# Where the first statistics, sums and normalizations stand ahead of the first w2 products

## The chip, the cores and the metric

The kernel runs on one core of one Trainium2 chip. A core has a matrix engine (TensorE, PE in the profile; its weight loads are listed apart as PEld), three engines for element work (VectorE or DVE, ScalarE or ACT, GpSimd or POOL), a queue that issues transfers (SyncE or SP), and 16 DMA engines. Each engine takes its instructions strictly in the order in which they were built, and waits at one whose inputs or whose buffer are not ready; what stands behind it waits too. The metric is the device time of a run in microseconds (us).

## The reference

The input x is 2048 x 576, in float32. It is normalized row by row, and two branches on the result are added to x:

```python
xn = _layernorm(x, axis=-1)
return x + _A_ref(xn, A_dft_seq_re, A_dft_seq_im, A_dft_hid_re, A_dft_hid_im) + _B_ref(xn, B_w1, B_w2)
# _A_ref:  a = xn @ dft_hid_re.T;  b = xn @ dft_hid_im.T;  y = dft_seq_re @ a - dft_seq_im @ b
# _B_ref:  h = max(xn @ w1, 0);    y = h @ w2              (w1: 576 x 4608, w2: 4608 x 576)
```

Branch A is a Fourier mixing written as matrix products; branch B is a two-layer perceptron with a rectifier.

## The kernel before

**Numbers.** PE multiplies float16. Every float32 operand is split into a high and a low float16 part, `split`: ACT writes the high part scaled by a power of two, then DVE writes the low part (lines 182 and 183). A product is the sum of three products of parts. The power of two comes from the largest magnitude of the operand: for the first block of weights DVE takes the maximum of each partition (`magnitude`, line 115, and line 575), PE transposes it (line 158), DVE reduces it (line 163), PE spreads it over the partitions (line 166), and DVE makes the scales with bit operations (lines 168 to 173).

**Stages.** x lies in 16 tiles of 128 rows, four tiles to a group. The hidden width 4608 is cut into 9 blocks of 512, and each step (block b, group g) computes the first layer for one block and one group, then the second. The second layer uses a scheme with seven products on quarters, whose operands are sums of quarters (`mlp1_out`, `sums_w2`). Results of the second layer are added into sums and written out by POOL with accumulating transfers (line 557). After all blocks comes branch A, which takes the last third of the time. The change touches only the opening: what happens before and around the first products with w2, that is steps (0, 0) and (0, 1).

**The opening, per tile t.** `stats` takes means and variances: two `bn_stats` on DVE per tile (line 200), an aggregate (line 203), a square root on ACT (line 210), and six small DVE operations (lines 211 to 222), the last of which is the shift `sh`. `normalize`, in the code N(t), writes the normalized tile in float32 on DVE (line 242) and its high part in float16 on ACT (line 243). `remainder`, E(t), subtracts the two for the low part (lines 247 and 250): on DVE for tile 0, on POOL for tiles 1 to 11. `transposes`, T(t), is ten transposes on PE into a PSUM buffer, and two copies by ACT into `xT` (lines 265 and 268). The PSUM pool of these buffers has two of them. One is held for a long stretch by the first two results of group 1 (`pq`); the transposes, the scale computations and later the w2 products take turns with what is left. `tile_by` is the first-layer products of one tile. `fill` is products whose result is not used. `sum_w2` sums magnitudes of w2 on ACT (line 630; the cast of the sums on DVE is line 640), and its scale leads to the splits of w2, which the first w2 product (line 540) needs. `mlp1_out` evacuates first-layer results: the rectified high parts on ACT (lines 350 and 353), low parts and sums on DVE (lines 354 to 358), then the high part of the sums on ACT (line 360) and the low part on DVE (line 361).

**What sets the order.** The kernel is written as one sequence of calls, from which a scheduler builds an order for each engine, by its own estimates; an instruction can move ahead of others on its engine where its inputs allow. `tc.issue_after(i)` keeps what is issued under it from being placed ahead of instruction i. Before the change this is used in the opening only for the statistics of tiles 12 to 15. `weave` mixes the steps of `stats` with other calls.

Of the kernel before, what the change touches and what calls it, by code (L numbers as in the profile page):

```python
# [13 lines left out]
AF = mybir.ActivationFunctionType  # L14
# [6 lines left out]
D = 576  # L21
# [28 lines left out]
def kernel(  # L50
# [139 lines left out]
    eps = const.tile([P, 1], F32, name="eps")  # L190
    nc.vector.memset(eps, EPS)

    def stats(ts):

        n = len(ts)
        mv = small.tile([P, n, 2], F32, tag=f"mv{n}", name=f"mv{ts[0]}")
        sts = [small.tile([P, 2, 6], F32, tag="st", name=f"st{t}", bufs=4) for t in ts]
        for t, st in zip(ts, sts):
            for j in range(2):
                nc.vector.bn_stats(st[:, j, :], acc[t][:, j * EH : (j + 1) * EH])  # L200
                yield
        for i, st in enumerate(sts):
            nc.vector.bn_aggr(mv[:, i], st.rearrange("p a b -> p (a b)"))
            yield
        r0, u, r, sh = (
            small.tile([P, n], F32, tag=f"{a}{n}", name=f"{a}_{ts[0]}") for a in ("r0", "u", "r", "sh")
        )
        m, v = mv[:, :, 0], mv[:, :, 1]
        stt = nc.vector.scalar_tensor_tensor
        nc.scalar.activation(u, v, AF.Sqrt, bias=eps)  # L210
        nc.vector.reciprocal(r0, u)
        yield

        stt(u, v, EPS, r0, ALU.add, ALU.mult)
        yield
        nc.vector.tensor_tensor(u, u, r0, ALU.mult)
        yield
        nc.vector.tensor_scalar(u, u, -0.5 * SX, 1.5 * SX, ALU.mult, ALU.add)
        yield
        nc.vector.tensor_tensor(r, u, r0, ALU.mult)  # L220
        yield
        stt(sh, m, -1.0, r, ALU.mult, ALU.mult)
        for i, t in enumerate(ts):
            means[t], factors[t], shifts[t] = mv[:, i, 0:1], r[:, i : i + 1], sh[:, i : i + 1]

# [8 lines left out]

    xns, xss = {}, {}

    def normalize(t, eng=nc.vector):
        stage = dbufs[t % 4]
        xn = xns[t] = stage[:, :D]

        xs = xss[t] = stage[:, D : 2 * D].bitcast(F16)
        eng.tensor_scalar(xn, acc[t], means[t], factors[t], ALU.subtract, ALU.mult)
        nc.scalar.activation(xs[:, :D], acc[t], AF.Identity, bias=shifts[t], scale=factors[t])  # L243

    def remainder(t, eng):
        xn, xs = xns[t], xss[t]
# [7 lines left out]
    def transposes(t):  # L254
        xs = xss[t]
        pt = ps2.tile([P, 2, 1024], F16, tag="ps2", name=f"pt{t}")
        for k in range(NKX):
            nc.tensor.transpose(
                pt[:, k // 8, (k % 8) * P : (k % 8 + 1) * P], xs[:, k * P : (k + 1) * P], ident
            )  # L260
        g, c = divmod(t, TG)

        nc.tensor.transpose(pt[:, 1, P : 2 * P], xs[:, D - P : D], ident)
        dst = xT[g][:, :, c * P : (c + 1) * P]
        nc.scalar.activation(
            dst[:, :8, :], pt[:, 0, :].rearrange("p (k t) -> p k t", t=P), AF.Copy
        )
        nc.scalar.activation(
            dst[:, 8:, :], pt[:, 1, : 2 * P].rearrange("p (k t) -> p k t", t=P), AF.Copy
        )  # L270

# [66 lines left out]
            ps.append(new_ps1(b, g, 0))  # L340
        mlp1_group(b, g, i, slice(0, G), ps[i], WK[:-1], start=(i == 0), stop=(i > 0))

    def mlp1_out(b, g, i, pa, pb):

        h = hs[b, g, i] = mlp.tile([P, 2, 7, GH], F16, tag="h", name=f"h{b}_{g}_{i}", bufs=4)
        st = mlp.tile([P, 5, GH], F32, tag="stage", name=f"s{b}_{g}_{i}")
        stt = nc.vector.scalar_tensor_tensor
        a11, a21, a12, a22 = pa[:, :GH], pa[:, GH:], pb[:, :GH], pb[:, GH:]
        r21, s1, s2, s3, s4 = (st[:, n] for n in range(5))
        nc.scalar.activation(r21, a21, AF.Relu)  # L350
        for q, src in ((slice(A11, A11 + 1), a11), (slice(A12, A22 + 1), pb)):
            hi, lo = (h[:, n, q].rearrange("p a b -> p (a b)") for n in range(2))
            nc.scalar.activation(hi, src, AF.Relu)
            stt(lo, src, 0.0, hi, ALU.max, ALU.subtract)  # L354
        stt(s3, a11, 0.0, r21, ALU.max, ALU.subtract)
        stt(s1, a22, 0.0, r21, ALU.max, ALU.add)
        stt(s2, a22, 0.0, s3, ALU.max, ALU.subtract)
        stt(s4, a12, 0.0, s2, ALU.max, ALU.subtract)
        hi, lo = (h[:, n, S1 : S4 + 1] for n in range(2))
        order["s"] = nc.scalar.activation(hi, st[:, 1:], AF.Copy).ins  # L360
        order["lo"] = nc.vector.tensor_tensor(lo, st[:, 1:], hi, ALU.subtract).ins  # L361
# [199 lines left out]
    def max_w1(b, f):  # L561

        i, r = divmod(f, 2)
        if f == 0:
            mx["w1", b], sc["w1", b], pw["w1", b] = cell("mw1"), cell("sw1"), cell("pw1")
        if r == 0:
            mx["f", b] = cell("mf", 2)
        with tc.issue_after(order["vfree"]) if b >= BB else nullcontext():
            magnitude(mx["f", b][:, r : r + 1], raws["w1", b, i][:, r * KT : (r + 1) * KT])
        if r:  # L570
            if b:
                m = mx["w1", b][:, i : i + 1]
            else:
                m = mx["b", i] = small.tile([P, 1], BF16, tag=f"mb{i}", name=f"mb{b}_{i}")
            nc.vector.tensor_reduce(m, mx["f", b], AX.X, ALU.max)
# [6 lines left out]
    def power_w1(b, i):  # L582
        s, p = (t["w1", b][:, i : i + 1] for t in (sc, pw))
        if b:
            yield from power(s, p, mx["w1", b][:, i : i + 1])
        else:
            power_pe(s, p, mx["b", i])
# [30 lines left out]
    def sum_w2(b, i):  # L618

        if i == 0:  # L620
            mx["w2", b], sc["w2", b], pw["w2", b] = cell("mw2"), cell("tw2"), cell("pw2")
        if b:
            junk = mlp.tile([P, 5, GH], F32, tag="stage", name=f"j{b}_{i}")
            junk = junk.rearrange("p a b -> p (a b)")[:, : 4 * EH]
            junk = junk.rearrange("p (q e) -> p q e", e=EH)
        else:
            new_w2(b, i)
            junk = w2s[b, i][:, 0, :4]
        with tc.issue_after(order["free"]) if b >= BB else nullcontext():
            nc.scalar.activation(  # L630
                junk, raws["w2", b, i], AF.Abs, scale=2.0**-10, accum_out=mx["w2", b][:, i : i + 1]
            )
# [133 lines left out]
    max_w1(0, 1)  # L766
    E(0, V)
    next(power_w1(0, 0), None)
    fill(24)
    T(0)  # L770
    fill(10, xss[0])
    split_w1(0, 0)
    tile_by(0, (0,), ps, WK0)
    split_w1(0, 1)
    tile_by(0, (1,), ps)
    weave(stats([1]))
    fill(8, xss[0])
    N(1)
    E(1, GP)
    T(1)  # L780
    fill(8, xss[1])
    s23 = stats([2, 3])
    weave(s23, no, lambda: max_w1(0, 2), no, lambda: max_w1(0, 3), lambda: next(power_w1(0, 1), None))
    tile_by(1, (0, 1), ps)
    split_w1(0, 2)
    N(2)
# [25 lines left out]
    T(6)  # L812
    tile_by(5, (0, 1), qs)
    T(7)
    weave(stats([8, 9, 10, 11]))
    for t in (8, 9, 10, 11):
        N(t)
        E(t, GP)
    mlp1_out(0, 0, 1, *ps[2:])
    tile_by(6, (0, 1), qs)  # L820
    w[3]()
    tile_by(7, (0, 1), qs)
# [424 lines left out]
```

## Time and profile before

| | |
|---|---|
| median of 3 runs | 1261.11 us (1260.76 to 1262.15) |
| profiled execution | 1262.99 us |
| its span on the core | 1261.1 us |
| PE busy | 1237.7 us |
| DVE busy | 1014.5 us |
| ACT busy | 716.9 us |
| POOL busy | 157.4 us |
| first w2 product starts | 58.77 us after the span's start |

How to read the rows below: a row of the timeline has its start, its duration, the engine, the line of the kernel before, the operation, what it writes and reads, and the shapes; "x4" merges four neighbours; a bracket at the end gives the time that the engine stood idle before it and what ended that. Instructions on an engine overlap a little, so the distance to the next start is less than the duration. In the chain of work that ended last a row has start, duration, and what the chain ran through.

### The profile page before, as it was taken

The numbers are of one execution on the slowest core, as the hardware profiler recorded it, in microseconds if no ns is written. First come the engines' busy times: TensorE is split into PE (matmuls) and PEld (weight loads), VectorE is DVE, ScalarE is ACT, GpSimd is POOL, SyncE is SP. The second block draws the span as 40 slices with busy tenths as digits, with TensorE's granted clock in tenths as the row PEclk, the third lists the DMA queues.
The fourth block names the chain that finished last, engine by engine and source line by source line (L and its number), as shares of the span: only waits on it lengthen the run. The fifth ranks groups of instructions, "written<-read, shape, count | busy, mean of one in ns | idle before, by whom it ended". The sixth has DMA issues, their size and how long they took to land.

```text
span 1261.1 us, 25526 instructions
## 1 busy us (share of the span) xinstructions
PE 1237.7 (98%) x10389; PEld 988.3 (78%) x10389; DVE 1014.5 (80%) x1921; ACT 716.9 (57%) x1210; POOL 157.4 (12%) x199
## 2 busy tenths in 40 slices
PE   8799999999999999999999999999999999999998
PEld 7565556888888888888888888877777777777776
DVE  8899987878878777788787878566888888787875
ACT  5866566676676666766766766544543433433342
POOL 2322211111111111212121212200000000000000
PEclk9999999999999999999999999999999999999999
DMA  9245657575657575756576766630054344434320
GB/s 339 80 81 95 122 117 157 116 134 136 133 123 171 120 154 116 136 139 135 118 160 134 156 127 120 116 84 1 1 172 124 124 125 142 144 109 145 117 87 20
DMA packets 65157, 155.46 MB, mean 123 GB/s; under 512 B 6544, under 2 KB 25488, under 8 KB 65040
## 3 DMA queue, kind: packets, MB, share of 16 engines
q1 hardware_dynamic: 42256, 111.36, 27.0%
q0 software_dynamic: 22784, 42.48, 25.1%
q8 instruction: 81, 1.33, 0.4%
q14 instruction: 36, 0.29, 0.1%
HBM read 106.63 MB, written 51.90 MB: 126 GB/s over the span
## 4 chain that ended last, share of the span: by engine, by line
PE 81%; DVE 10%; ACT 3%; DMA 3%; issue 2%; SPq 0%; POOL 0%; ACTq 0%; POOLq 0%; DVEq 0%
PE p L1179 24%; PE p L540 24%; PE bank L463 23%; PE pd L1060 8%; DMA raw_w<-in_w_dram 1%; PE p L310 1%; DVE w2s L183 1%; DVE h L361 1%; DMA acc<-in_x_dram 1%; DVE h L354 1%; DVE acc L409 1%; ACT w2s L182 1%; ACT dbuf L243 1%; DVE cs L183 0%; DVE dbuf L424 0%
## 5 line engine op out<-in xcount | busy, mean ns | idle before, releaser
L540 PE MATMUL p<-w2s,h 128*128 128x288 f16 x3024 | 408.2, 286 | 5.1 <-DVE acc L554 1.9
L540 PEld LDWEIGHTS <-h 128*128 128x128 f16 x3024 | 295.6, 98 | 80.6 <-issue 5.1
L1179 PE MATMUL p<-R,cs 128*128 128x288 f16 x2688 | 331.3, 287 | 2.3 <-DVE o L1185 2.3
L1179 PEld LDWEIGHTS <-cs 128*128 128x128 f16 x2688 | 263.7, 98 | 69.8 <-issue 2.5
L182 ACT ACTIVATE cs<-c,sc_c 128x1024 f16<-128x1024 f32 x112 | 128.2, 1148 | 196.2 <-PE p L1179 135.9
L183 DVE SCALAR_TENSOR_TENSOR cs<-c,sc_c,cs 128x1024 f16<-128x1024 f32 x112 | 143.4, 1282 | 41.3 <-ACT cs L182 40.9
L463 PEld LDWEIGHTS <-w1buf 128*128 128x128 f16 x1600 | 156.5, 98 | 21.6 <-issue 0.3
L463 PEld LDWEIGHTS <-dbuf 128*128 128x128 f16 x1200 | 117.4, 98 | 16.1
L463 PE MATMUL bank<-xT,w1buf 128*128 128x256 f16 x832 | 109.9, 273 | 0.0
L1060 PE MATMUL pd<-dbuf,xT 128*128 128x288 f16 x832 | 103.8, 286 | 0.0
L463 PE MATMUL bank<-acc,w1buf 128*128 128x256 f16 x768 | 102.1, 273 | 0.1
L1060 PEld LDWEIGHTS <-xT 128*128 128x128 f16 x832 | 80.8, 98 | 22.0 <-issue 1.9
L485 DVE TENSOR_TENSOR h<-s,h 128x1024 f16<-128x1024 f32 x56 | 68.5, 1223 | 33.9 <-ACT h L482 33.6
L557 POOL DMA_DIRECT2D spill<-dbuf x70 | 61.0, 875 | 234.2 <-DVE dbuf L554 202.6
L470 ACT ACTIVATE h<-acc 128x256 f16<-128x256 f32 x112 | 46.0, 411 | 76.7 <-DVE acc L493 71.4
L463 PE MATMUL bank<-xT,dbuf 128*128 128x256 f16 x624 | 82.5, 273 | 0.0
L482 ACT ACTIVATE h<-s 128x1024 f16<-128x1024 f32 x56 | 59.1, 1056 | 36.3 <-DVE s L477 35.6
L463 PE MATMUL bank<-acc,dbuf 128*128 128x256 f16 x576 | 76.6, 273 | 0.0
L1185 DVE SCALAR_TENSOR_TENSOR o<-p,us_c,o 128x288 f32<-128x288 f32 x112 | 57.5, 514 | 19.2 <-PE p L1179 19.2
L927 ACT ACTIVATE f<-f 128x1024 f32<-128x1024 f32 x64 | 66.9, 1046 | 0.4 <-DMA f<-in_cre_dram 0.3
L471 DVE SCALAR_TENSOR_TENSOR h<-acc,h 128x256 f16<-128x256 f32 x112 | 47.3, 422 | 20.6 <-ACT h L470 20.4
L551 ACT ACTIVATE dbuf<-p,c_ub 128x576 f32<-128x576 f32 x70 | 51.1, 731 | 15.2 <-PE p L540 14.9
(158 smaller groups left out, 1553.0 us busy)
## 6 DMA issues: line engine op xcount, KB each, us to landing
spill<-dbuf POOLq DMA_DIRECT2D x70, 288.0 KB, 5.3
f<-in_cre_dram SPq DMA_DIRECT2D x32, 512.0 KB, 5.5
f<-in_cim_dram SPq DMA_DIRECT2D x32, 512.0 KB, 5.0
c<-in_cre_dram SPq DMA_DIRECT2D x32, 512.0 KB, 4.4
c<-in_cim_dram SPq DMA_DIRECT2D x32, 512.0 KB, 4.8
spill<-sum POOLq DMA_DIRECT2D x42, 288.0 KB, 4.5
raw_w<-in_w_dram SPq DMA_DIRECT2D x17, 640.0 KB, 6.4
raw_w<-in_w_dram SPq DMA_DIRECT2D x18, 576.0 KB, 4.9
```

What stands on the lines that cost most here:

```text
L182: nc.scalar.activation(hi, src, AF.Copy, scale=s)
L183: nc.vector.scalar_tensor_tensor(lo, src, s, hi, ALU.mult, ALU.subtract)
L463: nc.tensor.matmul(ps, l, r, start=first and m == 0, stop=m == len(todo) - 1, skip_group_check=not first,)
L482: order["s"] = nc.scalar.activation(hi_s, st[:, 1:], AF.Copy).ins
L485: order["lo"] = nc.vector.tensor_tensor(lo_s, st[:, 1:], hi_s, ALU.subtract).ins
L540: nc.tensor.matmul(ps[:, c], h[:, x, qa, c * P : (c + 1) * P], w[:, y, qb], start=first and i == 0 and j == 0, stop=i == NQ - 1 and j == 2 ...
L551: freed(nc.scalar.activation(o, ps, AF.Copy, scale=us[b]))
L557: nc.gpsimd.dma_start(spill[g, row, col], o, accum_op=ALU.add)
L927: nc.scalar.activation(f, f, AF.Abs, scale=2.0**-10, accum_out=sums_c[:, n, q : q + 1])
L1060: nc.tensor.matmul(ps[j], xT[g][:, kx, c * P : (c + 1) * P], dsp[j][:, hl, k], start=(t % 2 == 0 and n == 0), stop=(t % 2 == 1 and n == le ...
L1179: nc.tensor.matmul(ps, w[:, a, k], r[:, c, rq], start=first and k == 0 and j == 0, stop=k == HK - 1 and j == 2, skip_group_check=not first,)
L1185: order["o"] = nc.vector.scalar_tensor_tensor(o, ps, us["c"][:, n : n + 1], o, ALU.mult, ALU.add).ins
```

## The change

A helper `behind(key)` holds an instruction behind one that was noted in `order`. Two kinds are now noted there: the last small step of `stats` (the shift, by its first tile) and the second copy of a tile's transposes (`xT`). With these, the opening is reordered:

- the statistics of tile 1 are called ahead of the split of the first w1 pair, and tile 1 is normalized ahead of its products;
- the maxima of the second w1 pair, and their scale, come after tile 1's shift and ahead of T(1), instead of in between the statistics of tiles 2 and 3; the statistics of tiles 2 and 3 are held behind tile 1's shift;
- the sums of w2 on ACT are held behind the copies of T(2) and T(3);
- the statistics of tiles 8 to 11 are held behind the shift of tiles 4 to 7;
- the ACT half of the normalization of tile 8 is held behind the copy of T(5), that of tiles 9 to 11 behind the copy of T(7), and the second evacuation of step (0, 0) on ACT behind the copy of T(6).

```diff
+    def behind(key):
+        return tc.issue_after(order[key]) if key in order else nullcontext()
-    def stats(ts):
+    def stats(ts, after=None):
...
-                nc.vector.bn_stats(st[:, j, :], acc[t][:, j * EH : (j + 1) * EH])
+                with behind(after):
+                    nc.vector.bn_stats(st[:, j, :], acc[t][:, j * EH : (j + 1) * EH])
...
-        stt(sh, m, -1.0, r, ALU.mult, ALU.mult)
+        order["sh", ts[0]] = stt(sh, m, -1.0, r, ALU.mult, ALU.mult).ins
...
-    def normalize(t, eng=nc.vector):
+    def normalize(t, eng=nc.vector, after=None):
...
-        nc.scalar.activation(xs[:, :D], acc[t], AF.Identity, bias=shifts[t], scale=factors[t])
+        with behind(after):
+            nc.scalar.activation(xs[:, :D], acc[t], AF.Identity, bias=shifts[t], scale=factors[t])
...
-        nc.scalar.activation(
+        order["xT", t] = nc.scalar.activation(
             dst[:, 8:, :], pt[:, 1, : 2 * P].rearrange("p (k t) -> p k t", t=P), AF.Copy
-        )
+        ).ins
...
-    def mlp1_out(b, g, i, pa, pb):
+    def mlp1_out(b, g, i, pa, pb, after=None):
...
-        nc.scalar.activation(r21, a21, AF.Relu)
+        with behind(after):
+            nc.scalar.activation(r21, a21, AF.Relu)
...
-            nc.scalar.activation(hi, src, AF.Relu)
+            with behind(after):
+                nc.scalar.activation(hi, src, AF.Relu)
...
-        with tc.issue_after(order["vfree"]) if b >= BB else nullcontext():
+        with behind("vfree" if b >= BB else ("sh", 1) if f > 1 else None):
             magnitude(mx["f", b][:, r : r + 1], raws["w1", b, i][:, r * KT : (r + 1) * KT])
...
-        with tc.issue_after(order["free"]) if b >= BB else nullcontext():
+        with behind("free" if b >= BB else None if b else ("xT", 2 + i)):
             nc.scalar.activation(
                 junk, raws["w2", b, i], AF.Abs, scale=2.0**-10, accum_out=mx["w2", b][:, i : i + 1]
             )
...
     next(power_w1(0, 0), None)
+    weave(stats([1]))
     fill(24)
     T(0)
     fill(10, xss[0])
     split_w1(0, 0)
     tile_by(0, (0,), ps, WK0)
     split_w1(0, 1)
-    tile_by(0, (1,), ps)
-    weave(stats([1]))
-    fill(8, xss[0])
     N(1)
     E(1, GP)
+    tile_by(0, (1,), ps)
+    fill(8, xss[0])
+    max_w1(0, 2)
+    max_w1(0, 3)
+    next(power_w1(0, 1), None)
     T(1)
     fill(8, xss[1])
-    s23 = stats([2, 3])
-    weave(s23, no, lambda: max_w1(0, 2), no, lambda: max_w1(0, 3), lambda: next(power_w1(0, 1), None))
+    weave(stats([2, 3], ("sh", 1)))
     tile_by(1, (0, 1), ps)
...
     T(7)
-    weave(stats([8, 9, 10, 11]))
-    for t in (8, 9, 10, 11):
-        N(t)
+    weave(stats([8, 9, 10, 11], ("sh", 4)))
+    N(8, after=("xT", 5))
+    E(8, GP)
+    mlp1_out(0, 0, 1, *ps[2:], after=("xT", 6))
+    for t in (9, 10, 11):
+        N(t, after=("xT", 7))
         E(t, GP)
-    mlp1_out(0, 0, 1, *ps[2:])
     tile_by(6, (0, 1), qs)
```

What the scheduler builds from this differs from the kernel before in the opening, and for a short way into the second step of block 0 and the first of block 1; the order of SP's transfers is the same. On ACT the square root of tile 1 now stands ahead of the copies of T(0), the sums of w2 ahead of the square root of tiles 4 to 7, and the high parts of tiles 8 to 11 together behind the copies of T(7). On DVE the eight `bn_stats` of tiles 8 to 11 stand behind the normalizations of tiles 4 to 7, and four evacuations of step (0, 1) stand between the small steps of the w2 scale. On PE the matmul of line 158 for the second w1 pair stands ahead of T(1). On POOL two reductions for block 1's scales move behind spill writes.

## The prediction

> **What bounds the kernel now.** I read the page's busy shares, then busy time by stretch, then what PE waited for in order of time, then the chain that ended last.
>
> ```profile
> PE 1237.7 (98%) x10389; PEld 988.3 (78%) x10389; DVE 1014.5 (80%) x1921; ACT 716.9 (57%) x1210; POOL 157.4 (12%) x199
> ```
> ```profile
> 0.00:60.00 60.00, 47.41 (x614) 39.59 (x615) 52.23 (x156) 42.39 (x71) 18.04 (x26) 0.97 0.61 209
> ```
> ```profile
> 66.00:118.00 52.00, 49.88 (x357) 32.57 (x355) 48.80 (x110) 34.81 (x57) 11.06 (x12) 1.00 0.48 75
> 118.00:191.00 73.00, 72.38 (x457) 43.66 (x457) 69.05 (x137) 41.78 (x72) 15.40 (x17) 1.00 0.62 120
> ```
> ```profile
> 58.77 1.02 PE L540 MATMUL p<-w2s,h 128*128 128x288 f16 x7 [0.96 <-ACT xT L268]
> ...
> 118.42 1.63 PE L540 MATMUL p<-w2s,h 128*128 128x288 f16 x12 [1.95 <-DVE acc L554]
> ```
> ```profile
> 99.23 1.60 DVE dbuf L183 x2
> 100.85 4.97 DMA raw_w<-in_w_dram
> ...
> 117.64 1.45 DVE acc L554 x2
> ```
> Columns of a stretch: its bounds and length, then busy PE, PEld, DVE, ACT, POOL, then clock and DMA. Over the span PE is full (98%), but the first 60 us have 12.6 us without PE work; there the kernel is a relay of DVE, ACT, POOL and PE. The first w2 product starts at 58.77. From 66 to 118 DVE is busy 94% of the time and PE 96%, and at 118.42 it is PE that waits, 1.95 us for DVE. The chain says why: a DVE split at 99.23 frees a buffer, a load of 4.97 follows, then the scale, then DVE work up to 117.64. All of this starts when DVE gets there. So two dates decide what the change is worth: when PE starts the w2 products (58.77), and when DVE has finished block 0's second tile group. PE has 1.95 us to spare against DVE at 118.42; a late DVE has nothing to spare.
>
> **The change, part one: tiles 1 to 3, and the start of 4 to 7.** Line numbers are those of the kernel before.
>
> ```profile
> 10.32 0.20 DVE L203 BATCH_NORM_AGGREGATE mv<-st 128x2 f32<-128x12 f32 x1
> ...
> 10.76 1.66 DVE L183 SCALAR_TENSOR_TENSOR w1buf<-raw_w,c_sw,w1buf 128x640 f16<-128x640 f32 x2
> ...
> 14.41 0.81 DVE L115 TENSOR_REDUCE c_mf<-raw_w 128x1 f32<-128x640 f32 x1
> ...
> 15.40 0.58 DVE L242 TENSOR_SCALAR dbuf<-acc,mv,r 128x576 f32<-128x576 f32 x1
> ...
> 20.47 0.56 DVE L242 TENSOR_SCALAR dbuf<-acc,mv,r 128x576 f32<-128x576 f32 x1
> ...
> 27.06 0.45 DVE L200 BATCH_NORM_STATS2 st<-acc 128x6 f32<-128x288 f32 x1
> 27.43 0.15 DVE L218 TENSOR_SCALAR u<-u 128x4 f32<-128x4 f32 x1
> ...
> 28.14 2.04 DVE L242 TENSOR_SCALAR dbuf<-acc,mv,r 128x576 f32<-128x576 f32 x4
> ```
> ```profile
> 16.48 1.15 ACT L630 ACTIVATE w2s<-raw_w 128x1152 f16<-128x1152 f32 x1
> ...
> 29.84 1.00 ACT L265 ACTIVATE xT<-pt 128x1024 f16<-128x1024 f16 x1
> 30.74 0.36 ACT L268 ACTIVATE xT<-pt 128x256 f16<-128x256 f16 x1
> 31.01 1.62 ACT L243 ACTIVATE dbuf<-acc,sh,r 128x576 f16<-128x576 f32 x2
> ```
> Up to the aggregate at 10.32 nothing moves. Then the two w1 splits (1.66) follow at once, and tile 1's small steps run back to back: from 10.44, 1.6 for the splits and about 1.0 for six steps that each wait for the one before. Tile 1 is normalized at 13.1, not 15.40: 2.3 us won. Its transposes win less, because in the new PE order the matmul on the second w1 scale stands ahead of them, and that scale now follows on DVE: 13.55 plus two reductions of 0.73 and a statistic of 0.37 (27.06 to 27.43) gives 15.4. So T(1) ends at 16.4, copied by 17.7.
>
> DVE then does four statistics, the scale, two aggregates, four more statistics, both splits of the second w1 pair, a ninth statistic: 13.55 + 1.46 + 4 x 0.37 + 0.7 + 4 x 0.37 + 2 x 0.79 + 0.37 + 0.4 of small steps = 21.0 for tiles 2 and 3, where the row has 20.47. So 0.6 lost there, while the second w1 split is done at 20.6.
>
> Here the first new wait bites. On ACT both sums of w2 now stand behind the copies of T(2) and T(3). Tile 2's ACT half runs 21.2 to 22.1, POOL's remainder to 23.6, T(2) to 24.05. Then ACT in order: copy 1.18, sum 1.2 (1.15 and its read-out), copy 1.18, sum 1.2, which is 28.8, and only then the square root for tiles 4 to 7. On DVE the cast of these sums (L640) stands ahead of that tile group's small steps, so DVE, free at 23.9, stands for 4.9 us. Six steps from 28.85 put the four normalizations at 30.2, where the row has 28.14: 2.0 us late, and the eight statistics of tiles 8 to 11 (8 x 0.37 = 3.0), done by then before, come after.
>
> One price here has no row: a reduction of DVE beside POOL's remainder of tile 1 (14.1 to 15.55). Of the rows beside POOL in the next fence but one, L355 reads one tensor in SBUF and is not held, L218 is held 0.9. I take nothing, since a reduction reads one tensor as L355 does; up to 1.0 late goes into the range.
>
> **Part two: the copies of T(5) to T(7).**
>
> ```profile
> 39.56 0.66 PE L258 MATMUL pt<-ident,dbuf 128*128 128x128 f16 x9 [2.60 <-ACT xT L268]
> ```
> ```profile
> 34.18 1.16 POOL L250 TENSOR_TENSOR dbuf<-dbuf 128x512 f16<-128x512 f32 x1
> 34.28 1.09 DVE L218 TENSOR_SCALAR u<-u 128x4 f32<-128x4 f32 x1
> ...
> 37.36 1.38 POOL L250 TENSOR_TENSOR dbuf<-dbuf 128x512 f16<-128x512 f32 x1
> ...
> 37.97 0.42 DVE L355 SCALAR_TENSOR_TENSOR s<-p,s 128x256 f32<-128x256 f32 x1
> ...
> 41.49 1.22 DVE L361 TENSOR_TENSOR h<-s,h 128x1024 f16<-128x1024 f32 x1
> ...
> 44.44 1.15 POOL L250 TENSOR_TENSOR dbuf<-dbuf 128x512 f16<-128x512 f32 x1
> ...
> 45.08 1.60 DVE L361 TENSOR_TENSOR h<-s,h 128x1024 f16<-128x1024 f32 x1 [1.57 <-ACT h L360]
> ```
> Before, T(6) waits 2.60 for T(5)'s copy, because ACT stood at tile 8's normalization. Now tile 8 comes behind that copy. ACT: four halves of tiles 4 to 7 from 30.27 (0.76 each) to 33.4, copy of T(4), two evacuations; T(5) leaves PE at 36.0, copied 37.3; T(6) starts at 37.5, not 39.56; 28 matmuls, T(7) at 39.75, copied 42.2. That is 2 to 4 us won on PE.
>
> It is given back to POOL's remainders of 8 to 11, which move behind it, to 43.5 and after: 4 x 1.47 = 5.9 us. The rows show what that does. L218 takes 0.15 alone and 1.09 beside POOL; L361 1.22 and 1.60. Both end as POOL's instruction ends. L355, whose one operand is PSUM, keeps 0.42. So DVE's normalizations, low parts and scale steps take turns with POOL; its PSUM evacuations do not. [...]
>
> Turn by turn from 43.5: POOL on tile 8 to 44.8; DVE tile 9's normalization to 45.3; evacuation; tile 10 to 46.1; POOL (9) to 47.1; tile 11 to 47.6; POOL (10) to 48.9; low part L361 to 50.0; POOL (11) to 51.25; then the w2 scale's steps, between which four evacuations of the next tile group now stand (0.33, 0.33, 0.60, 0.33).
>
> ```profile
> 46.69 0.41 DVE L163 TENSOR_REDUCE top<-pm 1x2 bf16<-1x256 f32 x1
> ...
> 49.19 0.23 DVE L652 TENSOR_SCALAR c_sw<-c_pw,c_inv 128x2 f32<-128x2 f32 x1
> ```
> The scale is ready at about 53.5, where the row has 49.42. Without any turn lost after tile 9 it is 51.15.
>
> **Part three: from the scale to the w2 products, and the sum.**
>
> ```profile
> 49.45 1.01 ACT L182 ACTIVATE w2s<-raw_w,c_sw 128x864 f16<-128x864 f32 x1 [0.45 <-DVE c_sw L652]
> 50.38 0.58 ACT L353 ACTIVATE h<-p 128x512 f16<-128x512 f32 x1
> ...
> 53.45 0.80 ACT L182 ACTIVATE w2s<-raw_w,c_sw 128x576 f16<-128x576 f32 x1
> ...
> 55.69 1.09 ACT L360 ACTIVATE h<-s 128x1024 f16<-128x1024 f32 x1
> ```
> ```profile
> 59.21 4.09 SPq L107 DMA_DIRECT2D raw_w<-in_w_dram  x2
> ```
> ```profile
> 63.53 0.81 DVE L115 TENSOR_REDUCE c_mf<-raw_w 128x1 f32<-128x640 f32 x1
> ...
> 65.80 1.23 DVE L361 TENSOR_TENSOR h<-s,h 128x1024 f16<-128x1024 f32 x1 [0.21 <-ACT h L360]
> ```
> ACT after the scale: two splits of 0.92, the high sums 0.95, T(9)'s copy 1.18, 0.47, T(10)'s first copy 0.91, a split 0.67, T(10)'s second copy 0.4: 6.45, and the first w2 product waits for that buffer. 53.5 + 6.45 = 60.0, against 58.77: 1.2 late. (Before it was 9.3 after the scale; the evacuations and T(8) now lie ahead of the scale, so part of the loss returns.)
>
> DVE from the scale's start at 53.3 has 14.3 us of work to the end of the second low part: three evacuations 1.0, two splits 2.1, eight sums 2.9, two low parts 2.3, four splits 2.9, evacuation 1.6, two reductions 1.46. The reductions need block 1's first w1 load, issued when the last split of the first w2 buffer ends, 62.3. Before, issue 59.21 to reduction 63.53 is 4.3 without a wait; now DVE asks 3.05 after the split: 0.8 to 1.3 of standing. End of the low part: 53.3 + 14.3 + 1.3 = 68.9 against 66.94 (65.80 and 1.14 to the next): 2.0 late.
>
> The later date decides. PE's 1.2 lies inside its 1.95 of spare time; DVE's 2.0 passes through the load at 100.85 to the wait at 118.42 and to the end, as after 118 both engines are full. SP issues the same transfers in the same order. On POOL the two reductions for block 1's w1 scales move behind the first and the fourth spill write:
> ```profile
> 69.22 1.40 POOL L557 DMA_DIRECT2D spill<-acc  x1 [3.12 <-DVE acc L554]
> ```
> At 1.40 each or less, plus the wait for the product, that costs nothing while the splits that need these scales stand some 15 us later (the second pair's at 99.23); without this cover it would be up to 3 x 1.40. Sum: +2.0. The profiled execution took 1262.99 around its span of 1261.1, so 1265.0 for it; it stands 1.88 above the median of the runs, 1261.11, so 1263.1 for the median. 0.2%, 2.5 us, is about what a measurement can tell from no change.
>
> **The rivals.**
> 1. The early copies win. PE has tile 7's transposes 4 us sooner; if POOL gets its turns during evacuations alone and the scale is ready by 49.4 as before, the first product is at 55.9 (2.9 early) and DVE, from 49.2, at 63.5 to 64.8, without and with the standing (3.4 to 2.1 early): 2.7 faster, 1258.4. For it: the 2.60 wait does go. Against: the two held rows above, and four evacuations ahead of the scale. It turns faster once the scale starts before 51.3 (51.3 + 15.6 = 66.9).
> 2. Slower by more: the load is the wall. If block 1's w1 takes 6.3 from issue to landing, as half of these do (row below), DVE stands 2.0 more: +4.0, 1265.1. The held reduction (+1.0) goes the same way.
> ```profile
> DMA to landing us min/median/max: 3.7/6.3/8.1
> ```
> Against: the same load before needed no more than 4.3.
> 3. The change is hidden: DVE's loss is made up in the idle time between 66 and 118 (52.00 less 48.80) and nothing is left: 1261.1. Against: most of that idle time follows the load at 100.85, which moves along.
>
> **How the numbers follow.** Forecast +2.0: 0.40 (its own range 1261.6 to 1264.8; 0.26 of it within 0.2%, 0.14 slower). Load as the wall: 0.28, slower. Early copies: 0.20 (0.18 faster, 0.02 within). Hidden: 0.12 (0.10 within, 0.02 faster). That gives faster 0.20, within 0.38, slower 0.42. The range runs from the early copies with part of the spread of their own (1257.8) to the load with part of the held reduction (1266.0).
>
> **What would show it.** Right: DVE idle some 5 us ahead of L640 near 24 to 29; T(6) near 37.5 without a long wait; DVE steps of 0.15 near 1 us long beside POOL between 44 and 52; the w2 scale near 53; the first w2 product near 60; DVE waiting about 1 us for block 1's w1. Wrong: a scale before 51, or a first product before 58; or statistics finished early, because the sums of w2 did not hold ACT.

## The result, and the profile after

| | before | after |
|---|---|---|
| median of 18 runs each, side by side | 1261.55 us (1259.41 to 1262.90) | 1265.10 us (1262.24 to 1270.06) |
| ratio, 95% interval | | 1.0030 (1.0022 to 1.0037) |
| profiled execution | 1262.99 us, span 1261.1 | 1266.75 us, span 1264.8 |
| mean granted clock of that execution | 0.997 | 0.995 |
| first w2 product starts | 58.77 | 60.46 |
| PE's wait for DVE near 120 ends | 118.42 | 121.42 |

The change makes the kernel 0.3% slower, 3.8 us by the ratio. The forecast was 1263.1 us, with a range of 1257.8 to 1266.0.

The timeline of DVE after the change. Line numbers are now those of the changed kernel: normalization is L247, the cast of the w2 sums L648, the w2 scale L660, the low part of the sums of quarters L369, an addition of a second-layer result L562.

```profile
12.58 0.58 DVE L247 TENSOR_SCALAR dbuf<-acc,mv,r 128x576 f32<-128x576 f32 x1
13.07 1.54 DVE L115 TENSOR_REDUCE c_mf<-raw_w 128x1 f32<-128x640 f32 x2
...
20.83 1.06 DVE L247 TENSOR_SCALAR dbuf<-acc,mv,r 128x576 f32<-128x576 f32 x2
...
28.66 0.17 DVE L648 CAST mb<-c_mw 128x2 bf16<-128x2 f32 x1 [5.36 <-ACT w2s L638]
...
29.94 2.05 DVE L247 TENSOR_SCALAR dbuf<-acc,mv,r 128x576 f32<-128x576 f32 x4
31.89 2.98 DVE L205 BATCH_NORM_STATS2 st<-acc 128x6 f32<-128x288 f32 x8
...
46.64 1.89 DVE L247 TENSOR_SCALAR dbuf<-acc,mv,r 128x576 f32<-128x576 f32 x2
...
51.35 1.05 DVE L652 TENSOR_TENSOR c_pp<-c_pw,c_pw 128x2 f32<-128x2 f32 x1
...
53.77 0.21 DVE L660 TENSOR_SCALAR c_sw<-c_pw,c_inv 128x2 f32<-128x2 f32 x1
...
66.79 1.55 DVE L115 TENSOR_REDUCE c_mf<-raw_w 128x1 f32<-128x640 f32 x2 [0.77 <-DMA raw_w<-in_w_dram]
68.25 1.22 DVE L369 TENSOR_TENSOR h<-s,h 128x1024 f16<-128x1024 f32 x1
69.38 1.17 DVE L205 BATCH_NORM_STATS2 st<-acc 128x6 f32<-128x288 f32 x3
71.17 0.82 DVE L562 SCALAR_TENSOR_TENSOR acc<-p,c_ub,acc 128x576 f32<-128x576 f32 x1 [0.61 <-PE p L548]
```

Read from the top: tile 1 is ready sooner (12.58), then DVE stands 5.36 us for the held sums of w2, then come tiles 4 to 7 and the eight statistics that before had been done by then. Between 45 and 52 DVE is held beside POOL, which works there from 44.64 to 52.39 with one gap of 0.49: two normalizations take 1.89 us, where the four at 29.94 take 2.05, and the short step of line 652 takes 1.05 and ends at 52.40, where the kernel before has 0.16. The scale is ready at 53.8. The low part of step (0, 1), counted to the start of the next instruction, ends at 69.38, against 66.94 before.

The timeline of PE:

```profile
38.59 0.67 PE L264 MATMUL pt<-ident,dbuf 128*128 128x128 f16 x9
...
58.12 0.66 PE L264 MATMUL pt<-ident,dbuf 128*128 128x128 f16 x9 [2.25 <-ACT xT L274]
...
60.46 1.84 PE L548 MATMUL p<-w2s,h 128*128 128x288 f16 x7 [1.62 <-ACT xT L274]
62.09 6.87 PE L316 MATMUL p<-xT,w1buf 128*128 128x512 f16 x28
...
121.42 3.04 PE L548 MATMUL p<-w2s,h 128*128 128x288 f16 x12 [2.10 <-DVE acc L562]
124.25 3.28 PE L316 MATMUL p<-xT,dbuf 128*128 128x512 f16 x13
```

T(6), at 38.59, no longer waits. But the seven first w2 products take 1.84 us where they took 1.02, and the twelve at 121.42 take 3.04 where they took 1.63: in this execution PE is slow right after it has stood, for 2.25 and 1.62 us ahead of the seven and for 2.10 ahead of the twelve. The same in busy time by stretch (the number behind the five engines is the granted clock):

```profile
30.00:35.00 5.00, 2.80 (x28) 2.46 (x29) 5.00 (x15) 4.34 (x7) 3.95 (x6) 0.77 1.00 289
35.00:40.00 5.00, 5.00 (x83) 5.00 (x81) 1.95 (x8) 3.28 (x8) 2.14 (x3) 0.89 0.41 134
55.00:60.00 5.00, 1.44 (x20) 1.20 (x20) 5.00 (x9) 5.00 (x8) 0.00 (x0) 1.00 0.02 3
60.00:65.00 5.00, 4.54 (x18) 2.23 (x18) 5.00 (x10) 3.58 (x7) 0.00 (x0) 0.66 0.20 48
...
119.00:121.40 2.40, 0.32 (x2) 0.04 (x1) 2.40 (x7) 2.37 (x4) 0.00 (x0) 1.00 0.00 0
121.40:124.00 2.60, 2.58 (x11) 1.57 (x11) 2.60 (x5) 0.83 (x2) 2.23 (x2) 0.51 0.35 23
```

PE is busy 1.44 of the five microseconds from 55 to 60, and from 60 to 65 it gets a clock of 0.66. It is busy 0.32 of 2.40 ahead of 121.4, and then gets 0.51.

### The profile page after: what moved, and what is told of

It is laid out like the page before. It is cut to its first block, busy times and chain, and to the rows that moved or that the text cites. A ratio compares the mean times of both kernels' runs of the same rounds, so it can differ in the third digit from the quotient of the medians.

```text
span 1264.8 us, 25525 instructions
## 1 busy us (share of the span) xinstructions
PE 1241.4 (98%) x10389; PEld 990.3 (78%) x10389; DVE 1013.6 (80%) x1921; ACT 718.1 (57%) x1210; POOL 158.2 (13%) x199
## 4 chain that ended last, share of the span: by engine, by line
PE 87%; DVE 6%; ACT 3%; issue 1%; DMA 1%; POOL 0%; SPq 0%; POOLq 0%; ACTq 0%; DVEq 0%
PE p L548 27%; PE p L1191 24%; PE bank L471 23%; PE pd L1072 8%; PE p L316 5%; ACT xT L271 1%; DVE cs L183 0%; DMA o<-spill 0%; DVE w2s L183 0%; ACT w2s L182 0%; DMA raw_w<-in_w_dram 0%; PE pd L1082 0%; DVE dbuf L247 0%; ACT f L939 0%; ACT h L368 0%
```

## The experiments: the change in its parts

All kernels were compared with the kernel before on their own chip, which gave medians of 1262.1 to 1262.3 us there; the ratios are to those runs. The change has three parts that can be taken apart: the order of tiles 1 to 3, the hold of the w2 sums behind T(2) and T(3), and the later places of tiles 8 to 11 and of the second evacuation.

**The sums not held.** The changed kernel, with one line as before:

```diff
-        with behind("free" if b >= BB else None if b else ("xT", 2 + i)):
+        with behind("free" if b >= BB else None):
```

> The changed kernel with one part undone: the sums of w2 on ACT are not held behind the copies of T(2) and T(3). The scheduler then puts both ahead of tile 2's normalization on ACT, and the square root of tiles 4 to 7 ahead of the copy of T(2). Theory A (the date at which DVE finishes the second low part of step (0, 1), 66.9 before and 69.4 after, passes to the end, and PE's clock adds to it): DVE no longer stands 5.4 us ahead of the cast, tiles 4 to 7 are normalized from about 25 instead of 29.9, and the low part ends 3 to 5 us sooner than after the change; the end at 1260.5 to 1262.5. Rival B (the loss is the lower PE clock after PE's waits at 55 to 60 and 119 to 121, not DVE's date): the waits of PE ahead of the first w2 product stay in kind, so 1264 to 1265.5. Rival C (the turns with POOL are the loss): these stay, so 1263.5 to 1265.

Measured: 1258.49 us, ratio 0.9965 (0.9953 to 0.9976). It is faster than both kernels. DVE:

```profile
23.66 0.49 DVE L648 CAST mb<-c_mw 128x2 bf16<-128x2 f32 x1
26.04 2.04 DVE L247 TENSOR_SCALAR dbuf<-acc,mv,r 128x576 f32<-128x576 f32 x4
...
43.03 0.70 DVE L660 TENSOR_SCALAR c_sw<-c_pw,c_inv 128x2 f32<-128x2 f32 x1
...
61.88 1.22 DVE L369 TENSOR_TENSOR h<-s,h 128x1024 f16<-128x1024 f32 x1
```

There is no stand ahead of the cast, tiles 4 to 7 are 3.9 us earlier, the scale 10.7 us. PE no longer waits for DVE near 120: the twelve products that stood at 121.42 start at 114.06 without a wait. By the ratios, this one hold costs 1.0030 less 0.9965, some 8 us, in the company of the other parts. Theory A has the direction right and underrates it; the two rivals fall.

**The order of tiles 1 to 3 alone.** The same, and tiles 8 to 11 and the second evacuation in their old places:

```diff
-    weave(stats([8, 9, 10, 11], ("sh", 4)))
-    N(8, after=("xT", 5))
-    E(8, GP)
-    mlp1_out(0, 0, 1, *ps[2:], after=("xT", 6))
-    for t in (9, 10, 11):
-        N(t, after=("xT", 7))
+    weave(stats([8, 9, 10, 11]))
+    for t in (8, 9, 10, 11):
+        N(t)
         E(t, GP)
+    mlp1_out(0, 0, 1, *ps[2:])
```

> The changed kernel with the sums of w2 not held and tiles 8 to 11 and the second evacuation of step (0, 0) in their old places: of the change, only the new order of tiles 1 to 3 is left. Theory A (the new places of the later tiles lose where the sums are held, since the statistics of tiles 8 to 11 then can no longer be done while DVE stands, and gain where they are free): no stand ahead of the cast, T(6) waits again about 2.6 us, scale at 45 to 47, low part 0 to 1.5 us earlier than 66.94, ratio to the kernel before 0.998 to 1.000 (1259.6 to 1262). Rival E (the order of tiles 1 to 3 is the whole gain of 0.9965 that the changed kernel without the hold has): ratio 0.996 to 0.9975.

Measured: 1259.38 us, ratio 0.9973 (0.9963 to 0.9984). That is rival E's range, though the interval just reaches theory A's (0.998): when the sums are free, the written places of the later tiles add nothing that can be told from zero. T(6), which I expected to wait again, starts at 35.46 without a wait.

```profile
26.81 2.04 DVE L247 TENSOR_SCALAR dbuf<-acc,mv,r 128x576 f32<-128x576 f32 x4
...
43.31 0.70 DVE L660 TENSOR_SCALAR c_sw<-c_pw,c_inv 128x2 f32<-128x2 f32 x1
...
62.25 1.22 DVE L369 TENSOR_TENSOR h<-s,h 128x1024 f16<-128x1024 f32 x1
```

But the gain is not that of the dates of tiles 1 to 3 alone. The scheduler moved the later tiles too, although nothing holds them here. On ACT the kernel before has tile 8's half ahead of the copy of T(5), and this run has it behind. First the kernel before (L243 the half, L265 the copy), then this run (L271 the copy, L249 the half):

```profile
35.94 0.87 ACT L243 ACTIVATE dbuf<-acc,sh,r 128x576 f16<-128x576 f32 x1 [1.41 <-DVE sh L222]
...
38.20 1.04 ACT L265 ACTIVATE xT<-pt 128x1024 f16<-128x1024 f16 x1
```

```profile
34.09 1.02 ACT L271 ACTIVATE xT<-pt 128x1024 f16<-128x1024 f16 x1
...
38.30 0.87 ACT L249 ACTIVATE dbuf<-acc,sh,r 128x576 f16<-128x576 f32 x1 [0.77 <-DVE sh L227]
```

Tiles 4 to 7 are normalized 1.3 us sooner than in the kernel before, but T(6) starts 4.1 us and the scale 6.1 us sooner. How much of the gain comes from either was not separated.

**The later tiles back, the sums held.** The edit shown last, made to the changed kernel with its hold:

> The changed kernel with tiles 8 to 11 (statistics, normalizations, remainders) and the second evacuation of step (0, 0) back in their old places. Theory A (most of the loss is the hold of the sums, the new place of the later tiles is worth little either way): DVE's stand of 5 us ahead of the cast stays, T(6) waits again about 2.6 us, the scale no longer takes turns with POOL but starts about 2 us later than 49.42, the second low part ends 1 to 2.5 us later than 66.94; time 1 to 3 us above the kernel before. Rival C (the later tiles' new place, with its turns between DVE and POOL, is the whole loss): low part within 0.5 of 66.94, the time within 0.5 us of the kernel before.

Measured: 1261.32 us, ratio 0.9994 (0.9985 to 1.0002). This is rival C: the low part starts at 65.89, against 65.80 in the kernel before, and the time cannot be told from that kernel's. With the hold in place, the later places cost 1.0030 less 0.9994, 4.5 us. Theory A's stand of 5 us is only 2.19, and the scale, at 46.63, comes earlier than 49.42, not later. The statistics of tiles 8 to 11 now fill the stand.

**The hold alone, in the kernel before:**

```diff
-        nc.scalar.activation(
+        order["xT", t] = nc.scalar.activation(
...
-        )
+        ).ins
...
-        with tc.issue_after(order["free"]) if b >= BB else nullcontext():
+        with tc.issue_after(order["free"] if b >= BB else order["xT", 2 + i]) if b >= BB or not b else nullcontext():
```

> The kernel before, with one part of the change alone: the sums of w2 on ACT held behind the copies of T(2) and T(3). Theory A (the hold makes DVE stand ahead of the cast of the sums, and the stand is passed on to tiles 4 to 7, the w2 scale and step (0, 1)): DVE idle 3 to 6 us ahead of the cast, tiles 4 to 7 normalized about 2 us later than 28.14, end of the second low part 1 to 2 us later than 66.94, 1 to 2.5 us slower than the kernel before. Rival B (the hold costs only together with the later tiles' new places): low part within 0.5 of 66.94, the time within 0.5 us of the kernel before.

Measured: 1262.81 us, ratio 1.0008 (0.9999 to 1.0017), so 0 to 2 us, which decides between neither theory. Theory A's stand does not appear: in this order the cast (30.86) comes behind eight more statistics and the normalization of tiles 4 to 7, so DVE has work while ACT is late. The low part still starts 0.9 us later than in the kernel before (66.74 for 65.80). What the hold costs depends on what DVE has left to do.

**The statistics of tiles 8 to 11 not held**, everything else as changed:

```diff
-    weave(stats([8, 9, 10, 11], ("sh", 4)))
+    weave(stats([8, 9, 10, 11]))
```

> The changed kernel, except that the statistics of tiles 8 to 11 are not held behind the shift of tiles 4 to 7. Theory A: they fill part of DVE's stand ahead of the cast, which falls from 5.36 to 2 to 3 us; after tiles 4 to 7 DVE has 3 us less to do, the scale is ready at 51 to 52.5 and the low part of step (0, 1) ends 1 to 2 us earlier than 69.38; ratio 0.9995 to 1.0015. Rival F (it is the turns between DVE and POOL and PE's clock that cost, and DVE has spare time after 30): scale within 0.5 of 53.77, ratio 1.002 to 1.004.

Measured: 1263.11 us, ratio 1.0006 (0.9998 to 1.0015): theory A, with the scale a little sooner than it had. DVE:

```profile
23.50 2.94 DVE L205 BATCH_NORM_STATS2 st<-acc 128x6 f32<-128x288 f32 x8
...
28.96 0.17 DVE L648 CAST mb<-c_mw 128x2 bf16<-128x2 f32 x1 [2.20 <-ACT w2s L638]
...
50.67 0.22 DVE L660 TENSOR_SCALAR c_sw<-c_pw,c_inv 128x2 f32<-128x2 f32 x1
```

The stand falls from 5.36 to 2.20 because the eight statistics (2.94) lie in it, and the scale is 3.1 us earlier. With the sums held, this second hold costs about 3 us (1.0030 less 1.0006). Also, tiles 8 to 11 are then normalized on DVE by 38.7, so that fewer of DVE's steps are left beside POOL's remainders at 45 to 49.

**POOL's remainders of tiles 9 to 11 left out**, to see what the turns with DVE cost:

```diff
     for t in (9, 10, 11):
         N(t, after=("xT", 7))
-        E(t, GP)
```

> The changed kernel with POOL's remainders of tiles 9 to 11 left out: the low parts of these three tiles are not computed, the transposes read what the buffers hold from earlier tiles, and the output is not the reference's for these rows. The order on ACT and DVE is that of the changed kernel. Theory A: the holds of DVE between 45 and 52.3 (0.7, 0.8, 0.6 and 0.9) go, the scale at about 51 instead of 53.8, the first w2 product at about 58, the low part at about 66.8, as before the change; the end at 1262 to 1263, the rest being PE's clock. Rival B: the waits of PE ahead of the products stay, so 1264.5 to 1265.5. Rival C (the turns with POOL are the whole loss): 1261 to 1261.7.

Measured: 1264.11 us, ratio 1.0012 (1.0004 to 1.0021), 2.3 us below the changed kernel by the ratios, and the scale is 1.6 us earlier (52.21). So leaving out the turns saves about 2 us. The time is in none of the three ranges, between theory A's and rival B's: the low part starts at 66.75, 1.0 us later than in the kernel before, but PE's wait near 120 ends at 120.85, 2.4 us later.

**The scale called early:**

```diff
     T(4)
+    w[3]()
...
     tile_by(6, (0, 1), qs)
-    w[3]()
     tile_by(7, (0, 1), qs)
```

> The changed kernel with the scale of w2 called after T(4) instead of after the products of tile 6. Its steps on DVE then stand between the normalizations and the statistics, while POOL works on tile 4, and the first w2 splits fill DVE's standing at 36.4 to 39.0. Theory A: the scale at about 34 instead of 53.8, the first w2 product at 55 to 57 instead of 60.5, the last low part of step (0, 1) 2 to 4 us sooner than 69.4; the end at 1261 to 1263. Rival B: as far as PE waits less ahead of the first products, 1.5 less: 1263.5. Rival C: the low part and the normalizations still take turns with POOL, only the scale steps' 1.5 goes: 1263.5.

Measured: 1265.18 us, ratio 1.0018 (1.0009 to 1.0026). Theory A's gain did not come; by the ratios the run is 1.5 us below the changed kernel, as rivals B and C had it, but the intervals overlap. The scale is ready at 39.33, 14 us earlier, but DVE then does the sums of w2 ahead of the low parts, and POOL's turns fall on them (POOL is busy for all of 50 to 55; in the changed kernel, with POOL idle, L670 takes 0.45 and L369 1.22):

```profile
51.15 1.41 DVE L670 TENSOR_TENSOR raw_w<-raw_w 128x288 f32<-128x288 f32 x1
...
52.81 2.10 DVE L369 TENSOR_TENSOR h<-s,h 128x1024 f16<-128x1024 f32 x1
...
69.66 1.23 DVE L369 TENSOR_TENSOR h<-s,h 128x1024 f16<-128x1024 f32 x1
```

The low part starts at 69.66, later than in the changed kernel (68.25), and yet the time is no longer. PE shows why:

```profile
61.61 1.84 PE L548 MATMUL p<-w2s,h 128*128 128x288 f16 x7 [0.81 <-ACT xT L274]
...
120.97 1.63 PE L548 MATMUL p<-w2s,h 128*128 128x288 f16 x12
```

The first w2 product comes 1.15 us later than in the changed kernel, and near 120 PE does not wait for DVE at all, so that the low part's date does not set the time there. So the date of the scale as such is not what the loss hangs on. The end of the low part sets the date near 120 only where PE waits for DVE there.

## The experiments: PE's clock

**PE kept busy** with 18 and 14 products whose result is not used, where the changed kernel stands for 2.25 and 1.62 us:

```diff
-        nc.tensor.transpose(pt[:, 1, P : 2 * P], xs[:, D - P : D], ident)
+        order["pt", t] = nc.tensor.transpose(pt[:, 1, P : 2 * P], xs[:, D - P : D], ident).ins
...
     T(10)
+    bank0 = new_ps1(0, 2, 0)
+
+    def keep(n, t):
+        for _ in range(n):
+            with tc.issue_after(order["pt", t]):
+                nc.tensor.matmul(
+                    bank0[:, :256], xss[9][:, :P], xss[9][:, :256], start=True, stop=True
+                )
+
+    keep(18, 10)
     T(11)
-    early = [mlp1(0, 2, 0), mlp1(0, 2, 1)]
+    keep(14, 11)
+    mlp1_group(0, 2, 0, slice(0, G), bank0)
+    early = [bank0, mlp1(0, 2, 1)]
```

> The changed kernel with 18 products whose result is not used between T(10) and T(11) and 14 between T(11) and the first w2 product (written to a bank that the next product starts anew), so that PE does not stand there; nothing else is moved in that stretch. Theory A: the granted clock stays at full from 58 to 65, the first seven w2 products take 1.0 instead of 1.84 and the 28 behind them 6.2 instead of 6.87, so PE is 1.5 ahead, but DVE's date stays at 69.4: PE's wait near 119 grows by about that, and the end moves by less than 0.7 us: 1264.4 to 1265.5. Rival B: the 1.5 passes to the end, with what the clock costs near 121 on top: 1261.5 to 1263.6. Rival C: as theory A.

Measured: 1264.90 us, ratio 1.0020 (1.0011 to 1.0030). The clock is 1.00 from 55 to 65, the first seven w2 products take 1.02, the 28 behind them 6.20, and DVE no longer waits for PE at L562. The ratio is 0.001 lower, which is some 1.2 us, but the intervals overlap. PE's wait near 120 still ends 2.6 us late:

```profile
120.98 1.63 PE L548 MATMUL p<-w2s,h 128*128 128x288 f16 x12 [1.85 <-DVE acc L562]
```

That is nearest to theory A, although the wait did not grow as it had it (1.85 for 2.10): PE, 1.0 us ahead of the changed kernel at 67.79, is only 0.2 ahead when it comes to the wait (119.1 for 119.3). So most of the loss, 0.20% of 0.30%, stays when PE has its full clock from 55 to 65; that the rest is the clock's is likely, but the times alone don't show it.

The same with POOL's remainders of tiles 9 to 11 left out:

```diff
     for t in (9, 10, 11):
         N(t, after=("xT", 7))
-        E(t, GP)
...
+    keep(18, 10)
     T(11)
...
+    keep(12, 11)
```

> The changed kernel without POOL's low parts of tiles 9 to 11 (they are not computed), and with 18 and 12 products whose result is not used behind the transposes of tiles 10 and 11. Without these products the low part of step (0, 1) was 1 us late, but PE's wait near 120 came 2.4 us late. Theory A (the difference is PE's lower clock at 60 to 65, passed on because DVE waits for the first product of PE): at full clock DVE's wait of 1.45 us for that product goes, PE's wait near 120 ends at 119.2 to 119.8, the time 0.4 to 1.2 us above the kernel before. Rival D (DVE's new order between 69 and 118 costs that itself): the wait still ends at 120.5 to 121, the time 1.5 to 2.5 us above the kernel before.

Measured: 1263.25 us, ratio 1.0006 (0.9997 to 1.0015). The time is theory A's, 0.8 us above the kernel before; the upper end of the interval, 1.9 us, still reaches rival D. The profiled execution does not decide it, since it is among the fastest of its kernel (1260.95 us; its wait near 120 ends at 117.50, sooner than either had it). Why it is so fast is worth a look. Up to the w2 scale DVE runs the same instructions in the same order as without the added products, yet not at the same time. First the execution without, then the one with:

```profile
30.52 2.04 DVE L247 TENSOR_SCALAR dbuf<-acc,mv,r 128x576 f32<-128x576 f32 x4
...
39.47 0.69 DVE L362 SCALAR_TENSOR_TENSOR h<-p,h 128x512 f16<-128x512 f32 x1 [2.25 <-ACT h L361]
...
52.21 0.22 DVE L660 TENSOR_SCALAR c_sw<-c_pw,c_inv 128x2 f32<-128x2 f32 x1
```

```profile
30.05 2.04 DVE L247 TENSOR_SCALAR dbuf<-acc,mv,r 128x576 f32<-128x576 f32 x4
...
37.71 0.69 DVE L362 SCALAR_TENSOR_TENSOR h<-p,h 128x512 f16<-128x512 f32 x1 [1.23 <-ACT h L361]
...
50.44 0.22 DVE L660 TENSOR_SCALAR c_sw<-c_pw,c_inv 128x2 f32<-128x2 f32 x1
```

The normalizations start 0.47 apart, the scales 1.77. In between lies PE's clock, again first without, then with:

```profile
30.00:35.00 5.00, 2.53 (x29) 2.02 (x27) 4.90 (x16) 3.77 (x5) 3.37 (x5) 0.80 1.10 326
35.00:40.00 5.00, 5.00 (x80) 5.00 (x79) 2.10 (x9) 3.45 (x9) 2.72 (x4) 0.86 0.28 102
```

```profile
30.00:35.00 5.00, 2.69 (x42) 2.35 (x43) 5.00 (x14) 4.49 (x7) 3.84 (x6) 1.00 1.05 308
35.00:40.00 5.00, 5.00 (x94) 5.00 (x92) 3.25 (x14) 4.46 (x11) 2.25 (x3) 1.00 0.39 130
```

PE waited in T(4) for 1.28, 0.28 and 0.89 us in the execution with the products, and no longer than 1.3, 0.3 and 0.9 in the one without, and yet the clock from 30 to 35 was 1.00 with and 0.80 without. Where it was 0.80, the evacuation at L362 and DVE's queue behind it, up to the scale, came another 1.3 us later.

**PE kept busy in both stretches**: 22 products ahead of T(4) were added to the 18 and 14, and T(4) was held behind them.

```diff
-    T(4)
+    for _ in range(22):
+        with tc.issue_after(order["pt", 3]):
+            last = nc.tensor.matmul(ps[3][:, 3 * P :], xss[3][:, :P], xss[3][:, :P], start=True, stop=True).ins
+    with tc.issue_after(last):
+        T(4)
```

> The changed kernel with products whose result is not used in both stretches in which PE stands: 22 ahead of the transposes of tile 4 (30 to 33), 18 and 14 behind those of tiles 10 and 11. If the lower clock at 30 to 40 (0.77 and 0.89 in the profiled execution) is what made T(5) to T(7) later than my prediction had them, and a part of the loss: clock 1.00 from 30 to 65, T(6) at 37.3 to 38.0, low part ending at 68 to 69.2, ratio 1.0005 to 1.0015, less spread between runs. If that clock costs nothing: as with the second stretch alone, ratio 1.0015 to 1.0025.

Measured: 1262.49 us, ratio 1.0008 (0.9996 to 1.0019), but as a test of the early clock it settles nothing. The products read a buffer that tile 7 also uses, so they waited until 33.62 and did not fill the stand (2.45 us); the clock was 1.00 in that execution all the same; and the new order of PE moved other work too, so that the low part started at 64.80, far earlier than expected, and PE did not wait for DVE near 120.

**The sums free and PE kept busy:**

```diff
-        with behind("free" if b >= BB else None if b else ("xT", 2 + i)):
+        with behind("free" if b >= BB else None):
...
+    keep(4, 10)
     T(11)
...
+    keep(20, 11)
```

> The changed kernel with the sums of w2 not held, and 4 and 20 products whose result is not used put behind the transposes of tiles 10 and 11, where PE otherwise stands for 2.18 us. If the lower clock after that stand (0.66 in 55 to 60, the 28 products of the first layer 7.79 us instead of 6.20) is paid in full, since PE no longer waits for DVE at 114: clock 1.00 from 50 to 65, 1.3 to 1.7 us faster than the run without these products, 1256.8 to 1257.2. If a later wait takes it up: 1258.2 to 1258.6, with a wait of about 1.5 us for DVE somewhere before 120.

Measured: 1256.73 us, ratio 0.9959 (0.9946 to 0.9972). By the medians that is 1.8 us below the same kernel without these products, as expected if the clock is paid in full; by the ratios it is 0.8 us, with five runs each and intervals that overlap, so the times alone don't settle it. The traces show the stand and the slow stretch gone. Stretches without the products, then PE with them:

```profile
50.00:55.00 5.00, 2.39 (x26) 1.67 (x25) 5.00 (x11) 5.00 (x9) 0.00 (x0) 1.00 0.06 11
55.00:60.00 5.00, 5.00 (x20) 2.13 (x18) 4.98 (x12) 1.45 (x3) 0.00 (x0) 0.66 0.71 239
```

```profile
52.19 2.35 PE L851 MATMUL p<-dbuf 128*128 128x256 f16 x20
54.54 0.53 PE L548 MATMUL p<-w2s,h 128*128 128x288 f16 x3
55.45 6.20 PE L316 MATMUL p<-xT,w1buf 128*128 128x512 f16 x28 [0.39 <-ACT xT L271]
```

Without them the 28 first-layer products behind the stand take 7.79 us. This is the fastest version found, 5.4 us below the kernel before on its chip by the medians.

## Why the prediction was right, and where its sum fell short

**The walk up to the low part held.** Tile 1 was put at 13.1 (12.58), tiles 2 and 3 at 21.0 (20.83), the stand at 4.9 us (5.36), tiles 4 to 7 at 30.2 (29.94), the scale at 53.5 (53.77), the first w2 product at 60.0 (60.46), DVE's wait for block 1's load at 0.8 to 1.3 (0.77), the end of the low part at 68.9 (69.38). The reductions beside POOL, priced at nothing, take 1.54 for two, 0.77 each, while POOL works from 13.66 to 15.08; the two at 66.79, with POOL idle, take 1.55: not held. That reading one tensor in SBUF is what spares them, as the price had it, no run shows: L218 reads one, too (`u<-u`), and took 1.09 for 0.15.

So the hold of the sums, the eight statistics left for later and the turns with POOL were the right mechanisms, and the experiments show each of them: 8 us for the hold in this company, 3 for the statistics, 2 for the turns (they overlap and don't add up). One reading of the rows was wrong: L361 at 45.08 does not end as POOL's instruction ends. That one ends at 45.59 and L361 at 46.68, so L361 was held only until 45.59 and then took its usual 1.1 us.

**What failed is the last step of the sum**, "DVE's 2.0 passes through the load at 100.85 to the wait at 118.42 and to the end, as after 118 both engines are full". The lag was 2.44 at the low part and 3.00 at the wait (121.42 against 118.42). At the next group of products it was 4.36 (124.25 against 119.89), since the twelve products took 2.83 to the next start instead of 1.47. At the end of the span it was 3.7. Two terms were missing:

- PE after a stand was priced at full clock. It ran at 0.51 from 121.4 to 124 in this execution; that alone is 1.4 us. "PE's 1.2 lies inside its 1.95 of spare time" fails in the same way: the stretch behind the first w2 product also ran slowly (6.87 for 6.20), and DVE waited 0.61 for its result (L562), about the growth from 2.44 to 3.00. In the profiled execution with PE kept busy there, that wait is gone and the lag does not grow: 2.75 at the low part, 2.56 at the wait. Behind the wait the clock is 1.00 in that execution too, though no products were added there.
- T(6) was put at 37.5 and came at 38.59, with PE at 0.77 and 0.89 from 30 to 40. In the run with the remainders left out and PE kept busy, whose profiled execution has a clock of 1.00 there, T(6) starts at 37.25. At the scale 0.3 of the 1.1 was left.

The forecast (1263.1) is 2.0 us short of the median (1265.1). Of these, 0.4 are the base: the prediction started from the median of three runs, 1261.11, and the median of 18 is 1261.55. How much of the rest is the clock on average is not shown. Over 18 runs the changed kernel's granted clock is 0.9952 in the mean, and 0.9962 to 0.9966 in three sets of 25 to 29 runs of the kernel before. If PE's 1238 us of work paid that difference in full, it would be 1.2 to 1.7 us. But it is not paid in full everywhere: with PE kept busy the mean is 0.9979, above that of the kernel before, and the time is still 0.20% longer. What that run leaves, 2.5 us (1.4 to 3.8), is close to the 2.0 that the prediction put on DVE.

The range held with some luck. The measured 1265.1 lies just above 1261.6 to 1264.8, which the prediction gave to its own mechanism. The upper end of the whole range was there for a late load and a held reduction, neither of which came; it covered a term that the sum did not have.

**The rivals.** The load as the wall gave almost the measured time (1265.1) by another mechanism: DVE stood 0.77 for the load, not 2.0 more. "The early copies win" fell for the change as it is: T(6) came 1 us earlier than before, and the scale at 53.8, far behind the 51.3 where it turns. With the sums free it holds: T(6) starts without a wait (34.79), the scale at 43.03 is ahead of 51.3, and the kernel is faster. That the change is hidden fell too.

**What the prediction had the wrong way round** is the worth of the first part. It counted tile 1 as 2.3 us won and tiles 2 and 3 as 0.6 lost, and then only followed the new wait. Without that wait, writing tiles 1 to 3 in the new order is worth 0.27%, together with what the scheduler then did with the later tiles: a gain that the hold, together with the held statistics, turned into a loss.

## What to carry to other kernels

An instruction held back on one engine was paid for here on the engine whose next instruction reads the result (ACT's sums, DVE's 5.36 us); look there for work that can fill the stand, and don't hold that work back too. A stand of PE cost its length and, in some executions, a lower clock behind it (down to 0.51 after 2.10 us), so a date for PE after a wait needs both terms. Where a change has several holds, price them apart: here a good reordering was hidden under one bad hold. And read the order that the scheduler built, since it may already do what a hold is meant to force, as with T(5)'s copy here.

## What the runs showed of the hardware

I had not expected that PE's clock is lower after stands of about 2 us, in some executions and not in others. After PE's wait near 120 the twelve products took 3.04 us after 2.10 (changed kernel), 2.25 after 2.18 (remainders left out) and 2.54 after 2.28 (statistics not held), and the clock from 118 to 124 was 0.79, 0.81 and 0.72. They took 1.63, at a clock of 1.00, after 1.85 (PE kept busy), 1.95 (kernel before) and 2.27 (remainders left out, PE kept busy). The waits in T(4), the longest of 1.28 to 1.30 us, went with a clock from 30 to 35 of 0.77 (changed kernel) and 0.80 (remainders left out), and of 1.00 (statistics not held; remainders left out, PE kept busy). What decides between the two, no run here settles.

Over all runs, filling the stands raised the mean granted clock in each of three pairs: from 0.9952 to 0.9979 for the changed kernel, from 0.9943 to 0.9977 with the remainders left out, and from 0.9976 to 0.9994 with the sums free.
